# Partial sums of spectral products and of right operands: from GpSimd additions on tiles in SBUF to accumulating transfers into DRAM

## The chip, the cores and the metric

The kernel runs on one core of a Trainium2 chip. The time is the device time of one execution in microseconds (us). Before the change three executions took 2755.38, 2753.51 and 2754.12 us, a median of 2754.12 us. The core's engines are TensorE (PE, with its weight loads as PEld), VectorE (DVE), ScalarE (ACT), GpSimd (POOL) and SyncE (SP); each works through its own queue in order and waits for the others by semaphores.

## What is computed

Two sublayers stand side by side, and their outputs are concatenated along the last axis: multi-query attention with 32 heads of width 32 over 2048 tokens, and a Fourier mixing layer, which is a DFT over the hidden axis followed by the real part of a DFT over the sequence axis.

```python
def _A_ref(x, wq, wk, wv, wo):
    q = (x @ wq).reshape(B, S, H, Dh).transpose(0, 2, 1, 3)
    k = x @ wk
    v = x @ wv
    scores = einsum("bhqd,bkd->bhqk", q, k) * (Dh ** -0.5)
    p = softmax(scores, axis=-1)
    o = einsum("bhqk,bkd->bhqd", p, v)
    return o.transpose(0, 2, 1, 3).reshape(B, S, H * Dh) @ wo

def _B_ref(x, dft_seq_re, dft_seq_im, dft_hid_re, dft_hid_im):
    a = einsum("bsd,ed->bse", x, dft_hid_re)
    b = einsum("bsd,ed->bse", x, dft_hid_im)
    return einsum("ts,bse->bte", dft_seq_re, a) - einsum("ts,bse->bte", dft_seq_im, b)

return concatenate([_A_ref(...), _B_ref(...)], axis=-1)    # S=2048, D=1024, float32
```

## The kernel before

**The work.** One program holds both sublayers, and TensorE takes turns between them. The attention runs in 32 units (4 blocks of 512 queries by 8 groups of 4 heads). A unit has 32 steps. In a step a *row* (two products of 512 columns into `pss`) gives scores whose maximum DVE takes (`nm`) and whose sum of exponentials ACT takes; a *column* (two products into `pst`) gives the transposed scores, which ACT turns into `p`. After some steps a *burst* multiplies several chunks of `p` with `v` into a bank `psb`. The method `pv` issues a burst whole, or in two halves (its argument `part`) with a row and a column in between.

Between rows and columns stand the *products* of the projections and of the mixing layer, all into two banks called `psb`. Each operand is split into a rounded high part and a low part (`rh`, `rl` for right operands, `mh`, `ml` for left ones), and each product is three matmuls: high by high, high by low, low by high. DVE makes the high parts (`rounded`, a TENSOR_REDUCE), GpSimd most low parts (a subtraction of 1.3 us).

**The seven products of Strassen's scheme.** The mixing layer's two DFTs (`stage_1`, `stage_2`) and most of the output projection (`stage_3`) are done as two-by-two block products with seven instead of eight block multiplications, listed in `PRODUCTS`. So many operands are sums or differences of two blocks, and each product is added to or subtracted from one or two blocks of the result.

- Sums of results: `gather` evicts a bank into a tile `h` (a ring of three, `NHR`), on DVE. The first product of a result block is stored as it is. For a later one SP loads the block's partial sum from DRAM into a tile `y` (a ring of four, `NY`), GpSimd adds or subtracts `h`, and SP stores `y` again. The intermediate `a` (result of stage 1) lives in `a_d`, that of stage 2 in `y_d` until its last addition, which is stored to the output.
- Sums of right operands: `sum_up` loads two blocks into the tiles `r0` and `r1`, GpSimd adds or subtracts them, and SP stores the result to a scratch in DRAM (`as_...` for stage 2, `ws_...` for stage 3). When TensorE needs the operand, `prepare` loads it from there. Right operands of stage 1 and all left operands are summed in SBUF, in `prepare`.

**What sets the order.** The order of every engine's queue is written out when the program is built, by a planner (`Plan`). Each piece of work is a task with a planned duration, an engine and a priority; `run` picks, for the engine that is free first, the ready task of least priority, and `finish` passes its planned end to the tasks that depend on it. The main loop places TensorE's rows, columns, bursts and products at the planned times at which their inputs are there. So a changed planned duration of one task moves instructions on all engines. The planner's figures (`MM`, `ISSUE`, `FLIGHT`, ...) only set the order; on the chip, semaphores decide. All calls go through one line of the class `Ordered`, so nearly all rows of the profile have line L58, and one tells them apart by tiles.

Of the kernel before, what the change touches and what calls it, by code (L numbers as in the profile page):

```python
# [12 lines left out]
ALU = mybir.AluOpType  # L13
# [4 lines left out]
P = 128  # L18
S = 2048
D = 1024  # L20
H = 32
DH = 32
W = 512
# [20 lines left out]
EXTRA = 2  # L44
OVER = {"act": 0.1, "dve": 0.08, "pool": 0.06, "sp": 0.0}
LAG = {"act": 0.1, "dve": 0.1, "pool": 0.15, "sp": 0.3, "pe": 0.1}
ISSUE, RATE, FLIGHT = 0.42, 300.0, 3.0


class Ordered:  # L50
# [16 lines left out]
class Plan:  # L67
# [6 lines left out]
        self.port = {"dve": 0.0, "pool": 0.0}  # L74
        self.seq, self.dma = 0, 0.0

    def task(self, engines, us, emit, deps=(), prio=0.0, kb=0, order=(), into=None, port=False):
        if isinstance(engines, str):
            engines = ((engines, 0.0),)
        t = into or Task()  # L80
        t.engines, t.us, t.emit, t.prio, t.kb, t.port = engines, us, emit, prio, kb, port
        self.seq += 1
        t.seq = self.seq
        for kind, ds in ((0, deps), (1, order)):
            for d in ds:
                if d is None:
                    continue
                if d.end is None:
                    t.n += 1
                    d.outs.append((t, kind))  # L90
                else:
                    t.ready = max(t.ready, d.start if kind else d.end)
        if t.n == 0:
            self.learn(t)
        return t
# [23 lines left out]
    def run(self, until):  # L119
        while True:  # L120
            best = self.next()
            if best is None or best[0] > until:
                return
            at, e = best
            r, t = min((x for x in self.known[e] if x[0] <= at), key=lambda x: (x[1].prio, x[1].seq))
            for f, _ in t.engines:
                self.known[f] = [x for x in self.known[f] if x[1] is not t]
            t.on = e
            t.emit(e) if len(t.engines) > 1 else t.emit()
            us = t.us[e] if isinstance(t.us, dict) else t.us  # L130
            if e == "pool" or (e == "dve" and t.port):
                at = max(at, self.port["dve" if e == "pool" else "pool"])
                self.port[e] = at + us - OVER[e]
            end = at + us
            self.free[e] = max(end - OVER[e], at + us / 2)
            if e == "sp":
                self.dma = max(self.dma, end) + t.kb / RATE
                end = self.dma + FLIGHT
            self.finish(t, at, end)


class Slot:
# [45 lines left out]
def tile_kernel(ctx: ExitStack, tc, xT, wq, wkv, wo, xbT, wT, cT, out):  # L188
# [8 lines left out]
    plan = Plan()  # L197
# [62 lines left out]
    def maker(ring, *a, **k):  # L260
        t = plan.task(*a, order=ring.maker, **k)
        ring.maker = [t]
        return t
# [87 lines left out]
    def gather(g, at, outs, neg=False):  # L351

        s = hr.take()

        def evict():
            h = hr.make(s)
            if neg:
                dve.tensor_scalar_mul(h, g.ps, -1.0)
            else:
                dve.tensor_copy(h, g.ps)  # L360
        e = g.freed = maker(hr, "dve", 0.69, evict, deps=[g.done, *s.deps], prio=-0.5)
        for sg, key, n, to, of in outs:
            if of is None and sg > 0:
                s.users.append(store(to, lambda: s.tile, [e], at, key=(*key, n)))
                continue
            if of is None:
                s2 = hr.take()
                g.freed = maker(hr, "dve", 0.69, lambda s2=s2: dve.tensor_scalar_mul(hr.make(s2), g.ps, -1.0),
                                deps=[g.done, *s2.deps], prio=-0.5)
                s2.users.append(store(to, lambda s2=s2: s2.tile, [g.freed], at, key=(*key, n)))  # L370
                continue
            ys = yr.take()
            ld = plan.task("sp", ISSUE, lambda ys=ys, of=of: sp.dma_start(yr.make(ys), of()),
                           deps=[landed[*key, n - 1], *ys.deps], prio=at - 30, kb=256, order=yr.maker)
            yr.maker = [ld]
            f = gp.tensor_add if sg > 0 else gp.tensor_sub
            ad = plan.task("pool", 1.33, lambda ys=ys, f=f: f(ys.tile, ys.tile, s.tile), deps=[e, ld], prio=at - 20)
            s.users.append(ad)
            ys.users.append(store(to, lambda ys=ys: ys.tile, [ad], at, key=(*key, n)))

    def stage_1():
        seen = {}
# [22 lines left out]
    def stage_2():  # L405
        seen = {}
        for p in ORDER_2:
# [4 lines left out]
            for m in range(8):  # L412
# [3 lines left out]
                for i, j, sg in outs:  # L416
                    n = seen[i, j, m] = seen.get((i, j, m), 0) + 1
                    r0 = (i * 8 + m) * P
                    to = out[r0:r0 + P, D + j * W:D + (j + 1) * W] if n == TOTAL[i, j] else y_d[i][j][m]
                    got.append((sg, ("y", i, j, m), n, lambda to=to: to,  # L420
                                (lambda i=i, j=j, m=m: y_d[i][j][m]) if n > 1 else None))
                yield Group(L, R, lambda g, at, got=got: gather(g, at, got))

    def wo_set(e):
# [162 lines left out]

    def sum_up(it, at):

        slots = [raw["r"][a].take() for a in range(2)]  # L590
        t = [None, None]
        loads = []
# [602 lines left out]
```

## Time and profile before

| | before |
|---|---|
| median of three executions | 2754.12 us |
| the profiled execution, its own time | 2754.33 us |
| its span, first to last instruction | 2752.5 us |
| granted TensorE clock, mean | 0.999 |
| stage 1: first to last store of `a` begins | 353.6 to 1028.1 us |
| stage 2: first load of `y` to the last addition on `y` begins | 1063.7 to 2478.9 us |

The span leaves out 1.8 us around the first and last instruction. Busy shares are of the span; a matmul's end is modelled, so that matmuls which follow each other closely overlap in the records, and the spacing of their starts says more than their durations: products of 512 columns start every 0.23 us. Issuing a DMA does not count as busy time of an engine.

### The profile page before, as it was taken

What the parts mean: (1) busy time and instruction counts of PE and PEld (TensorE: products, weight loads), DVE (VectorE), ACT (ScalarE), POOL (GpSimd) and SP (SyncE); (2) the same over time, 40 slices, a digit from 0 to 9 for tenths busy, and PEclk for the clock granted to TensorE, in tenths of its full rate; (3) what the DMA queues carried; (4) which work ended last, traced back from release to release, by engine and by line L of the source; (5) the groups of instructions that cost most, each with busy time, mean ns of one, the idle gap of its engine ahead of it and who ended that gap; (6) DMA issues with size and microseconds to landing.
All of it is one profiled execution on the core that took longest, in us unless ns stands there. A gap on an engine that the chain in (4) does not pass through costs nothing.

```text
span 2752.5 us, 40883 instructions
## 1 busy us (share of the span) xinstructions
PE 2736.0 (99%) x13832; PEld 1930.3 (70%) x13832; DVE 1944.1 (71%) x2277; ACT 2199.5 (80%) x3197; POOL 1579.5 (57%) x1307
## 2 busy tenths in 40 slices
PE   9999999999999999999999999999999999999999
PEld 6777676767676767677677676676676776766766
DVE  8977676768777776676677677677677676678752
ACT  6688887878787878888888888888888888887631
POOL 2644245557776557556346356557768767555562
PEclk9999999999999999999999999999999999999999
DMA  9645366567786548547437445547858857444585
GB/s 279 210 135 159 104 202 207 191 231 256 249 257 222 169 149 281 171 133 250 141 106 249 143 136 174 154 153 254 272 182 279 278 161 238 127 127 153 160 277 176
DMA packets 337043, 536.48 MB, mean 195 GB/s; under 512 B 36800, under 2 KB 89536, under 8 KB 336832
## 3 DMA queue, kind: packets, MB, share of 16 engines
q1 hardware_dynamic: 336832, 533.87, 61.3%
q8 instruction: 108, 1.77, 0.3%
q14 instruction: 103, 0.84, 0.1%
HBM read 390.86 MB, written 141.82 MB: 194 GB/s over the span
## 4 chain that ended last, share of the span: by engine, by line
PE 97%; ACT 1%; DVE 1%; DMA 1%; issue 0%; POOL 0%; SPq 0%; ACTq 0%; DVEq 0%
PE psb L58 62%; PE pss L58 18%; PE pst L58 17%; ACT pss L58 0%; ACT p L58 0%; DMA qst<-in_xT_dram 0%; DVE h L58 0%; DMA ql<-y 0%; DVE nm L58 0%; DVE rl L58 0%; DMA m<-in_wkv_dram 0%; DVE y L58 0%; ACT h L58 0%; POOL rl L58 0%; DVE p L58 0%
## 5 line engine op out<-in xcount | busy, mean ns | idle before, releaser
L58 DVE TENSOR_REDUCE nm<-pss 128x1 f32<-128x1024 f32 x1024 | 1241.6, 1221 | 325.0 <-PE pss L58 321.2
L58 ACT ACTIVATE p<-pst 128x1024 f32<-128x1024 f32 x1024 | 1052.5, 1028 | 448.6 <-PE pst L58 397.7
L58 ACT ACTIVATE pss<-pss,nm 128x1024 f32<-128x1024 f32 x1024 | 1110.7, 1085 | 35.0 <-DVE nm L58 33.6
L58 POOL TENSOR_TENSOR ml<-m,mh 128x512 fp32r<-128x512 f32 x371 | 482.6, 1301 | 508.2 <-DVE mh L58 290.9
L58 PE MATMUL psb<-rl,mh 128*128 128x512 f32 x1732 | 683.3, 395 | 0.6 <-POOL rl L58 0.6
L58 PE MATMUL psb<-rh,mh 128*128 128x512 f32 x1732 | 683.7, 395 | 0.2 <-DVE y L58 0.2
L58 PE MATMUL psb<-rh,ml 128*128 128x512 f32 x1732 | 683.3, 394 | 0.0
L58 PE MATMUL pss<-kst,qst 128*128 128x512 f32 x2048 | 650.4, 398 | 0.9 <-ACT pss L58 0.9
L58 PE MATMUL pst<-qst,kst 128*128 128x512 f32 x2048 | 642.8, 395 | 2.4 <-ACT p L58 2.2
L58 PEld LDWEIGHTS pss<-kst,qst 128*128 128x128 f32 x2048 | 375.6, 188 | 163.6 <-issue 72.9
L58 PE MATMUL psb<-p,v 128*32 128x512 f32 x4096 | 461.8, 596 | 2.7 <-DVE h L58 2.7
L58 PEld LDWEIGHTS pst<-qst,kst 128*128 128x128 f32 x2048 | 382.5, 188 | 103.1 <-ACT p L58 8.6
L58 POOL TENSOR_TENSOR m<-m,m 128x512 f32<-128x512 f32 x230 | 301.0, 1309 | 152.4 <-DMA m<-in_cT_dram 93.8
L58 PEld LDWEIGHTS psb<-rh,mh 128*128 128x128 f32 x1732 | 324.9, 188 | 77.7 <-DVE y L58 0.6
L58 PEld LDWEIGHTS psb<-rl,mh 128*128 128x128 f32 x1732 | 324.9, 188 | 76.6 <-POOL rl L58 1.0
L58 PEld LDWEIGHTS psb<-rh,ml 128*128 128x128 f32 x1732 | 324.9, 188 | 75.7
L58 POOL TENSOR_TENSOR y<-y,h 128x512 f32<-128x512 f32 x192 | 249.3, 1306 | 176.8 <-DVE h L58 165.1
L58 PEld LDWEIGHTS psb<-p,v 128*32 128x32 f32 x4096 | 122.7, 110 | 286.5 <-issue 273.7
L58 POOL TENSOR_TENSOR rl<-r,rh 128x512 fp32r<-128x512 f32 x198 | 255.7, 1299 | 117.6 <-DVE rh L58 108.5
L58 DVE TENSOR_REDUCE mh<-m 128x512 fp32r<-128x512 f32 x371 | 250.7, 676 | 20.5 <-PE psb L58 13.8
L58 ACT ACTIVATION_READ_ACCUMULATOR pss<-pss,nm 128x1 f32 x1024 | 208.2, 203 | 0.0
L58 POOL TENSOR_TENSOR r<-r,r 128x512 f32<-128x512 f32 x140 | 180.5, 1293 | 47.8 <-DMA r<-a 31.1
(78 smaller groups left out, 977.0 us busy)
## 6 DMA issues: line engine op xcount, KB each, us to landing
m<-in_cT_dram SPq DMA_DIRECT2D x384, 256.0 KB, 3.8
r<-a SPq DMA_DIRECT2D x192, 256.0 KB, 4.2
y<-a SPq DMA_DIRECT2D x128, 256.0 KB, 3.7
a<-y SPq DMA_DIRECT2D x128, 256.0 KB, 3.2
r<-in_wT_dram SPq DMA_DIRECT2D x96, 256.0 KB, 3.9
m<-in_xbT_dram SPq DMA_DIRECT2D x96, 256.0 KB, 3.3
y<-y SPq DMA_DIRECT2D x96, 256.0 KB, 4.1
as<-r SPq DMA_DIRECT2D x80, 256.0 KB, 4.4
```

What stands on the lines that cost most here:

```text
L58: return lambda *a, **k: self.tc.keep_in_program_order(f(*a, **k))
```

## The change

In `gather` the load into `y`, the addition on GpSimd and the store are replaced by one transfer that GpSimd issues: it takes the tile `h` from SBUF and adds it to the block in DRAM (`accum_op=ALU.add`). Since it only adds, a product that is subtracted is evicted a second time, negated, into another tile `h`. The partial sums of stage 2 go to the output itself from the first product on, so that `y_d` is no longer used. In `sum_up` a sum with a plus sign becomes a copy from DRAM to DRAM that SP issues and an accumulating transfer from DRAM to DRAM on GpSimd; sums with a minus sign stay as they were. The planner gets a figure `ACC` for an issue on GpSimd, and `after`, a time by which a task's planned end lies behind the engine's part of it.

```diff
-ISSUE, RATE, FLIGHT = 0.42, 300.0, 3.0
+ISSUE, RATE, FLIGHT, ACC = 0.42, 300.0, 3.0, 1.0
...
-            self.finish(t, at, end)
+            self.finish(t, at, end + t.after)
...
-            ys = yr.take()
-            ld = plan.task("sp", ISSUE, lambda ys=ys, of=of: sp.dma_start(yr.make(ys), of()),
-                           deps=[landed[*key, n - 1], *ys.deps], prio=at - 30, kb=256, order=yr.maker)
-            yr.maker = [ld]
-            f = gp.tensor_add if sg > 0 else gp.tensor_sub
-            ad = plan.task("pool", 1.33, lambda ys=ys, f=f: f(ys.tile, ys.tile, s.tile), deps=[e, ld], prio=at - 20)
-            s.users.append(ad)
-            ys.users.append(store(to, lambda ys=ys: ys.tile, [ad], at, key=(*key, n)))
+            if sg < 0:
+                s2 = hr.take()
+                e2 = g.freed = maker(hr, "dve", 0.69, lambda s2=s2: dve.tensor_scalar_mul(hr.make(s2), g.ps, -1.0),
+                                     deps=[g.done, *s2.deps], prio=-0.5)
+            else:
+                s2, e2 = s, e
+            s2.users.append(plan.task("pool", ACC, lambda s2=s2, to=to: gp.dma_start(to(), s2.tile, accum_op=ALU.add),
+                                      deps=[e2, landed[*key, n - 1]], prio=at - 20, into=landed[*key, n], after=FLIGHT + 1.0))
...
-                    to = out[r0:r0 + P, D + j * W:D + (j + 1) * W] if n == TOTAL[i, j] else y_d[i][j][m]
+                    to = out[r0:r0 + P, D + j * W:D + (j + 1) * W]
                     got.append((sg, ("y", i, j, m), n, lambda to=to: to,
-                                (lambda i=i, j=j, m=m: y_d[i][j][m]) if n > 1 else None))
+                                True if n > 1 else None))
...
     def sum_up(it, at):
 
+        kept, key = it.sums, (it,)
+        if it.srcs[1][1] > 0:
+            (ap, _), (bp, _) = it.srcs
+            plan.task("sp", ISSUE, lambda: sp.dma_start(kept, ap(), max_dma_last_dim=2048), deps=[landed[it.after[0]] if it.after else at_group[at - 480].done],
+                      prio=at - 100, kb=256, into=landed[key, 0])
+            plan.task("pool", ACC, lambda: gp.dma_start(kept, bp(), accum_op=ALU.add, max_dma_last_dim=2048),
+                      deps=[landed[key, 0], *(landed[k] for k in it.after)], prio=at - 100, into=landed[key], after=FLIGHT + 1.0)
+            it.after, it.srcs = [key], [(lambda: kept, 1)]
+            return
```

Counted in the two programs, instruction by instruction:

| engine | what | before | after |
|---|---|---|---|
| PE | all instructions | 11786 | 11786 |
| PE | bursts on `p` and `v` that stand as one piece, or as a half | 102 | 96 |
| POOL | additions `y<-y,h` | 192 | 0 |
| POOL | sums `r<-r,r` | 140 | 80 |
| POOL | low parts `ml`, `rl` | 569 | 575 |
| POOL | accumulating transfers | 0 | 252 (192 from `h`, 60 from DRAM) |
| DVE | negated evictions `h<-psb` | 56 | 80 |
| DVE | low parts `ml<-m,mh`, `rl<-r,rh` | 69 | 63 |
| SP | issues and the like | 2238 | 1734 |

The planner gives other places to many instructions from about 350 us on. Three places follow.

**GpSimd, in stage 1**, where product 3 of `PRODUCTS` (counted from 0) is added to two result blocks at a time (`a_...` are the blocks in DRAM, `m0`, `m1` and `r0`, `r1` operands that are being summed). Before:

```order
L58 TENSOR_TENSOR y_6312<-y_6312,h_6513 128x512
L58 TENSOR_TENSOR y_6379<-y_6379,h_6513 128x512
L58 TENSOR_TENSOR m0_6436<-m0_6436,m1_6441 128x512
L58 TENSOR_TENSOR y_6478<-y_6478,h_6553 128x512
L58 TENSOR_TENSOR y_6510<-y_6510,h_6553 128x512
L58 TENSOR_TENSOR ml_6573<-m0_6198,mh_6572 128x512
```

And after, at the same place:

```order
L58 DMA a_0_1_0_198<-h_6461 128x512
L58 DMA a_1_1_0_230<-h_6461 128x512
L58 TENSOR_TENSOR ml_6473<-m0_6156,mh_6472 128x512
L58 TENSOR_TENSOR r0_6350<-r0_6350,r1_6405 128x512
L58 DMA a_0_0_1_183<-h_6511 128x512
L58 DMA a_1_0_1_215<-h_6511 128x512
L58 TENSOR_TENSOR rl_6533<-r0_6350,rh_6532 128x512
```

Each addition on a tile `y` has become one issue that reads `h`; both users of one `h` stand next to each other as before, and low parts and operand sums stand between them.

**TensorE, at the end of stage 1** (about 1000 us before the change): one burst. Before, in two halves with a row and a column between them:

```order
L58 MATMUL psb<-rl,mh 128x512
L58 MATMUL psb<-rh,ml 128x512
L58 MATMUL psb<-p,v 32x512 x12
L58 MATMUL pss<-kst,qst 128x512 x2
L58 MATMUL pst<-qst,kst 128x512 x2
L58 MATMUL psb<-p,v 32x512 x12
```

And after:

```order
L58 MATMUL psb<-rl,mh 128x512
L58 MATMUL psb<-rh,ml 128x512
L58 MATMUL psb<-p,v 32x512 x24
L58 MATMUL pss<-kst,qst 128x512 x2
L58 MATMUL pst<-qst,kst 128x512 x2
```

The two halves of 12 have become one burst of 24; the same happens at all six places where a burst stood in halves.

**TensorE, at the end of the attention** (from about 2630 us on). Before, the last columns stand where the products have run out; the last burst and the first output product (`pss<-rh,mh`) follow:

```order
L58 MATMUL pst<-qst,kst 128x512 x2
L58 MATMUL psb<-rh,ml 128x512
L58 MATMUL pst<-qst,kst 128x512 x4
L58 MATMUL psb<-p,v 32x512 x20
L58 MATMUL pss<-rh,mh 128x512
```

After, two columns stand back to back (x4) some 210 rows ahead of the last burst, in the second half of `stage_3`:

```order
L58 MATMUL pst<-qst,kst 128x512 x2
L58 MATMUL psb<-rh,mh 128x512
L58 MATMUL pst<-qst,kst 128x512 x4
L58 MATMUL psb<-rl,mh 128x512
L58 MATMUL psb<-rh,ml 128x512
```

while behind the last column 23 product matmuls are left, of which the last three stand here ahead of the last burst:

```order
L58 MATMUL psb<-rh,mh 128x512
L58 MATMUL psb<-rl,mh 128x512
L58 MATMUL psb<-rh,ml 128x512
L58 MATMUL psb<-p,v 32x512 x20
L58 MATMUL pss<-rh,mh 128x512
```

The pair of columns without a product between them has moved from the very end to a place further ahead.

More of the change, by code (lines that the diff above doesn't have):

```diff
@@ L75, in __init__, with task @@
         self.seq, self.dma = 0, 0.0
-    def task(self, engines, us, emit, deps=(), prio=0.0, kb=0, order=(), into=None, port=False):
+    def task(self, engines, us, emit, deps=(), prio=0.0, kb=0, order=(), into=None, port=False, after=0.0):
         if isinstance(engines, str):
@@ L80, in task @@
         t = into or Task()
-        t.engines, t.us, t.emit, t.prio, t.kb, t.port = engines, us, emit, prio, kb, port
+        t.engines, t.us, t.emit, t.prio, t.kb, t.port, t.after = engines, us, emit, prio, kb, port, after
         self.seq += 1
```

## The prediction

> **What bounds the kernel now.** I read the page's busy shares and its chain first.
>
> ```profile
> PE 2736.0 (99%) x13832; PEld 1930.3 (70%) x13832; DVE 1944.1 (71%) x2277; ACT 2199.5 (80%) x3197; POOL 1579.5 (57%) x1307
> PE 97%; ACT 1%; DVE 1%; DMA 1%; issue 0%; POOL 0%; SPq 0%; ACTq 0%; DVEq 0%
> ```
>
> TensorE is idle for 2752.5 - 2736.0 = 16.5 us, and 97% of the chain that ended last is its own. GpSimd and SP, where the change removes work, have no share of it. A busy PE need not be a dense one, so I looked next at what it waits for, over the whole span:
>
> ```profile
> engine line waited for: us in total, times, longest us
> PE psb L58 <- ACT p L58: 4.8, 1, 4.8
> PE psb L58 <- DVE h L58: 2.7, 4, 0.7
> PE pst L58 <- ACT p L58: 2.2, 3, 1.2
> PE pss L58 <- ACT pss L58: 0.9, 2, 0.7
> PE psb L58 <- DVE p L58: 0.9, 1, 0.9
> PE psb L58 <- POOL rl L58: 0.6, 1, 0.6
> PE psb L58 <- DVE y L58: 0.2, 1, 0.2
> ```
>
> That is 12.3 us. The waits of 4.8 and 0.9 on `p` are in the first 60 us, ahead of everything that the change moves. The one wait on GpSimd is 0.6 us. So all additions that leave GpSimd cost TensorE at most that now. The change has the same 11786 instructions on TensorE, so it can gain only by their order and by some 6 us of later waits; it can lose much more, if a new transfer comes late.
>
> **Term 1: six bursts in one piece, -2.0 us.** The order has 102 pieces of bursts before and 96 after. Two stretches price a piece; the number behind x counts records, two for each matmul:
>
> ```profile
> 1000.61 0.62 PE L58 MATMUL pst<-qst,kst 128*128 128x512 f32 x2
> 1001.16 2.78 PE L58 MATMUL psb<-p,v 128*32 128x512 f32 x24
> 1003.88 0.73 PE L58 MATMUL pss<-kst,qst 128*128 128x512 f32 x2
> 1004.44 0.62 PE L58 MATMUL pst<-qst,kst 128*128 128x512 f32 x2
> ...
> 1314.00 5.36 PE L58 MATMUL psb<-p,v 128*32 128x512 f32 x48
> 1319.29 0.73 PE L58 MATMUL pss<-kst,qst 128*128 128x512 f32 x2
> ```
>
> A half of 24 records takes 2.72 us from start to the next start, a whole burst of 48 takes 5.29; two halves are 0.15 us longer. The pair of matmuls ahead of a burst takes 0.55 us and the one behind it 0.56, instead of 2 x 0.23 = 0.46, which adds 0.09 + 0.10. A split costs 0.34 us, six of them 2.0 us.
>
> **Term 2: one transpose less ahead of a burst, -0.7 us.** All four waits on `h` above are of this kind: a small transpose takes a bank, and a burst behind it waits for the other bank's eviction.
>
> ```profile
> 1024.41 0.27 PE L58 MATMUL psb<-ident,m 128*128 128x128 f32 x1
> 1025.36 2.78 PE L58 MATMUL psb<-p,v 128*32 128x512 f32 x24 [0.68 <-DVE h L58]
> ```
>
> In the order this pair stands four times before, three times after: -0.7 us.
>
> **Term 3: the back-to-back columns, 0.** The end of the attention before:
>
> ```profile
> 2694.19 0.62 PE L58 MATMUL pst<-qst,kst 128*128 128x512 f32 x2
> 2694.65 0.40 PE L58 MATMUL psb<-rh,ml 128*128 128x512 f32 x1
> 2695.92 0.72 PE L58 MATMUL pst<-qst,kst 128*128 128x512 f32 x2 [0.88 <-ACT p L58]
> 2697.82 1.11 PE L58 MATMUL pst<-qst,kst 128*128 128x512 f32 x2 [1.17 <-ACT p L58]
> ```
>
> With one product between them these columns start 1.73 us apart, without one 1.90; there is only one tile `pst`, which ACT must empty. Dense, the starts would be 0.69 and 0.46 apart, so that 1.04 + 1.44 = 2.5 us are lost. After the change 23 products, 5.3 us, stand behind the last column, and this loss is gone from the end. But the same pattern (a column, one product, two columns) now stands some 210 rows earlier, for the same 2.5 us. I count 0, between -2.5 (should inputs on the chip space the earlier pair out anyway) and +1.2 (the wait of 0.6 on `rl`, which falls in the same half of stage 3, once or twice more).
>
> **Term 4: GpSimd's issues, 0.** The prices, and the densest stretch, by all work and by that on `y` alone:
>
> ```profile
> L58 POOL TENSOR_TENSOR y<-y,h 128x512 f32<-128x512 f32 x192 | 249.3, 1306 | 176.8 <-DVE h L58 165.1 <-DMA y<-a 6.9 <-issue 2.1
> L58 POOL TENSOR_TENSOR r<-r,r 128x512 f32<-128x512 f32 x140 | 180.5, 1293 | 47.8 <-DMA r<-a 31.1 <-DMA r<-in_wT_dram 9.6 <-DMA r<-in_wo_dram 2.1
> 600.00:700.00 100.00, 100.00 (x516) 69.44 (x515) 74.12 (x92) 80.56 (x120) 70.11 (x59) 1.00 0.72 236
> 700.00:800.00 100.00, 100.00 (x497) 72.28 (x495) 78.03 (x84) 86.07 (x125) 76.73 (x63) 1.00 0.81 258
> 800.00:900.00 100.00, 99.33 (x515) 69.46 (x514) 71.26 (x83) 78.70 (x114) 67.24 (x55) 1.00 0.71 228
> ...
> 600.00:700.00 100.00, 0.00 (x0) 32.98 (x26) 1.00 0.72 236
> 700.00:800.00 100.00, 0.00 (x0) 40.42 (x32) 1.00 0.81 258
> 800.00:900.00 100.00, 0.00 (x0) 31.66 (x24) 1.00 0.71 228
> 702.12 0.32 SPq L58 DMA_DIRECT2D y<-a  x1
> ```
>
> GpSimd loses 192 x 1.306 + 60 x 1.293 = 328 us and gains six low parts (7.8 us) and 252 issues. No row shows an issue by GpSimd. From below SP's 0.32 us bounds it; from above nothing does, so I take the price at which it begins to hurt: between 700 and 800 us GpSimd does 76.7 - 40.4 = 36.3 us of other work, and 32 issues fill the rest at 63.7 / 32 = 2.0 us each. I take 1.3, the nearest row of its own; then GpSimd is as busy as now, and TensorE waits no more than now. At 0.32 it would gain at most the 0.6 us.
>
> A queue effect comes with it. An accumulating transfer from DRAM waits in GpSimd's queue for SP's copy to land, and low parts wait behind it. The additions that it replaces already wait for landings (31.1 us on `r<-a` in the row above), and TensorE felt 0.6. Twice that is +0.6, inside the range.
>
> **Term 5: DVE, 0; SP, 0.**
>
> ```profile
> L58 DVE TENSOR_SCALAR h<-psb 128x512 f32<-128x512 f32 x56 | 38.4, 687 | 12.5 <-PE psb L58 12.0 <-issue 0.4 <-POOL y L58 0.2
> L58 DVE TENSOR_TENSOR rl<-r,rh 128x512 fp32r<-128x512 f32 x54 | 57.5, 1067 | 2.0 <-ACT rh L58 1.5
> L58 DVE TENSOR_TENSOR rl<-qst,rh 128x512 fp32r<-128x512 f32 x6 | 3.9, 682 | 1.5 <-ACT rh L58 1.5
> ```
>
> DVE gets 24 negated evictions, 16.5 us, and loses four low parts of 1.07 and two of about that, some 6 us. The other 10 us lie in its 808 idle us; without that cover they would be +10 us. SP issues 504 fewer DMAs at 0.32 us and more, which nothing waits for.
>
> **Term 6: the DMA engines, 0.**
>
> ```profile
> q1 hardware_dynamic: 336832, 533.87, 61.3%
> y<-a SPq DMA_DIRECT2D x128, 256.0 KB, 3.7
> a<-y SPq DMA_DIRECT2D x128, 256.0 KB, 3.2
> as<-r SPq DMA_DIRECT2D x80, 256.0 KB, 4.4
> ```
>
> 533.87 MB took 61.3% of 2752.5 us, so 256 KB take 0.83 us of all sixteen engines. 192 loads, 192 stores and 60 sums of three transfers go, 564; 60 copies and 252 accumulates come. From below an accumulate costs one such transfer. From above I again take the price that hurts: between 700 and 800 us, 64 of the replaced transfers are 53 of the 81 busy us, and 32 accumulates fill the 72 us that are then free at 2.25 us each, 2.7 transfers. I take two transfers, since an accumulate must read the block in DRAM that the load of `y` read: the load stays unchanged (312 - 252 + 504 = 564).
> The Trainium skill, "Collectives: The Full Stack", section "The bandwidth ceiling", says that an adding DMA is slower than a copying one because of its second read, not because of the addition, at about half the rate. By one transfer the stretch would be 55% loaded, and I would halve the chance of the DMA rival below; by that rule it is 81% loaded; the sum is 0 by either, and no run here shows it yet.
> As for time to land, an `h` is evicted every 6 us there (two users of each, 32 in 100 us), and the ring has three, so that a landing may take 15 us before DVE waits; SP's take 3 to 5.
>
> **Sum.** 2754.33 (the profiled execution's own time, 1.8 over its span and 0.2 over the median) - 2.0 - 0.7 = 2751.6 us.
>
> **The rivals.** *Slower: GpSimd becomes the bound of stage 1.* It decides from 2.0 us per issue. At 2.5, the three stretches above need 37.1 + 65.0 = 102, 36.3 + 80.0 = 116 and 35.6 + 60.0 = 96 of 100 us: +18 us, 2770; at 3.0 they need 115, 132 and 108: +55 us, 2806. For it speaks that a GpSimd instruction pays when DVE reads two operands from SBUF: the same subtraction takes DVE 682 ns at the start and 1067 later, beside a busy GpSimd. Had every issue to sit out one DVE instruction (78.03 / 84 = 0.93 us), it would be 1.3 + 0.9 = 2.2 us: 7 us over in the middle stretch, 2759. Against it: most of DVE's work there are reductions and evictions from PSUM.
> The Trainium skill, "SBUF — State Buffer", section "Who interferes with whom", says that descriptor generation on GpSimd is starved while DVE is in a two-port mode, and that reductions never are. By that rule the price stays near 1.3, since copies here come from PSUM; with it failing for every instruction it is the 2759 above. No run here shows it yet.
> Chance 0.13.
>
> *Slower: an accumulate holds the DMA engines for over 2.7 transfers.* At three (2.5 us) the three stretches come to 29 + 65, 28 + 80 and 31 + 60: +8 us, 2760; at four, +60 us, 2812. Against it: only these 300 us are so dense. Two transfers leave a margin of 2.7 / 2 = 1.35 before it decides; for that, chance 0.07. With a small remainder for a late operand elsewhere (+6 to +10, such as DVE's 10 us uncovered) 0.03.
>
> *Faster: every wait behind the first 60 us goes as well.* Term 3 gives -2.5, the other three transposes -2.0, `rl`, `pss` and `y` -1.6: 2751.6 - 6.1 = 2745.5. It needs all of them; half of them are enough to pass -0.2%. Against it: the pattern of columns is there in the new order. Chance 0.16.
>
> That the additions stay is no rival: the order shows none on `y`.
>
> **How the numbers follow.** The forecast, 2748.6 to 2759.6, has 0.61. About 0.2%, 5.5 us, is what a measurement of this kernel can tell from no change; so faster 0.16, same 0.61, slower 0.13 + 0.07 + 0.03 = 0.23. The range goes from 2746, nearly all of the gains, to 2770, GpSimd at 2.5 us per issue; about 0.12 lie above it and 0.05 below.
>
> **What would show it.** Terms 1 and 2: TensorE's waits on `h` at three times 0.7 us, no burst of 24 records, and 2730 to 2735 us busy. Term 3: starts of columns 1.7 to 1.9 us apart with no product between them some 70 us before the last burst, and none at the end. Term 4: the spacing of GpSimd's issues below 2 us; a wait of TensorE on `rl` or `ml` of more than a few us in stage 1 would prove it wrong. Term 6: a DMA share of at most about 0.8 in the densest stretch, and a share of the whole near 61%; far less would mean that an accumulate costs one transfer, and a full stretch that it costs three.

## The result and the profile after

The changed kernel takes 2774.35 us (median of 4, 2773.15 to 2775.13), the kernel before beside it 2754.75 us. The ratio is 1.0073, with a 95% interval from 1.0061 to 1.0085: 20 us slower, and outside the range of the prediction. Two executions of later versions, at a granted clock of 0.85 and 0.67, are left out of all medians and ratios.

The page of the changed kernel: its span, busy time by engine, DMA share in 40 slices, the queues' shares (queue, packets, MB, share of sixteen engines' span), and the chain by engine.

```profile
span 2773.4 us, 40227 instructions
PE 2741.3 (99%) x13832; PEld 1932.4 (70%) x13832; DVE 1946.5 (70%) x2295; ACT 2197.0 (79%) x3197; POOL 1485.8 (54%) x1313
DMA  9644356769999989647534336566557447445486
q1 hardware_dynamic: 264256, 401.72, 46.8%
q0 software_dynamic: 36288, 66.08, 16.3%
PE 91%; DMA 3%; POOL 2%; DVE 1%; ACT 1%; issue 1%; SPq 0%; POOLq 0%; ACTq 0%; DVEq 0%
```

GpSimd lost 94 us of busy time, as intended. TensorE's part of the chain fell from 97 to 91%, and DMA, which had 1%, has 3. In the slices the row of nines between 620 and 970 us is new. TensorE's waits (what it waited for: us in total, times, longest):

```profile
PE pst L58 <- ACT p L58: 9.9, 6, 3.9
PE pss L58 <- ACT pss L58: 8.7, 9, 2.3
PE psb L58 <- ACT p L58: 5.3, 1, 5.3
PE psb L58 <- DVE h L58: 3.3, 4, 1.3
...
```

With two small ones left out here they sum to 27.8 us, against 12.3 before. None of them names a DMA or GpSimd: it is mostly rows and columns that stand still, not products. The stretches of 100 us show where, and a second loss with it (columns as in the prediction: busy time of PE, PEld, DVE, ACT, POOL, then granted clock, DMA share, GB/s):

```profile
600.00:700.00 100.00, 94.88 (x465) 67.01 (x464) 69.55 (x85) 76.23 (x113) 65.97 (x64) 0.98 0.85 189
700.00:800.00 100.00, 93.16 (x472) 62.41 (x471) 71.09 (x80) 72.29 (x105) 59.90 (x60) 0.97 0.95 203
800.00:900.00 100.00, 97.34 (x482) 69.28 (x481) 70.29 (x82) 82.47 (x121) 66.50 (x65) 1.00 0.95 213
900.00:1000.00 100.00, 99.92 (x514) 69.02 (x514) 68.36 (x81) 81.14 (x118) 63.16 (x63) 1.00 0.95 209
```

TensorE is idle for 14.6 us between 600 and 900 us (0.7 before), and the granted clock is 0.98 and 0.97 in the first two stretches, which is (0.02 + 0.03) x 100 = some 5 us more of lost work. The DMA engines are busy for 85 to 95% where they were at 72, 81, 71 and 55%; up to 900 us they nevertheless move fewer bytes per second.

How a late load becomes a standing column is seen in the chain that ended last (start, us, what), here of the changed kernel ahead of its longest stall in stage 1:

```profile
758.65 7.52 DMA r<-in_wT_dram
...
767.66 7.07 DMA r<-in_wT_dram
...
780.35 0.21 POOL md L58
...
780.72 1.01 ACT p L58
...
781.78 1.22 PE pst L58 x2
```

Two loads that follow each other take 7.5 and 7.1 us, where the median of their kind is 4.2 and was 3.9 before. GpSimd works in order, so all that stands behind the late operand, down to the small `md` that ACT's exponential needs, comes late, and the column on `pst` has waited 3.88 us.

### The profile page after: what moved, and what is told of

It is laid out like the page before. It is cut to its first block, busy times and chain, and to the rows that moved or that the text cites. A ratio compares the mean times of both kernels' runs of the same rounds, so it can differ in the third digit from the quotient of the medians.

```text
span 2773.4 us, 40227 instructions
## 1 busy us (share of the span) xinstructions
PE 2741.3 (99%) x13832; PEld 1932.4 (70%) x13832; DVE 1946.5 (70%) x2295; ACT 2197.0 (79%) x3197; POOL 1485.8 (54%) x1313
## 3 DMA queue, kind: packets, MB, share of 16 engines
q1 hardware_dynamic: 264256, 401.72, 46.8%
q0 software_dynamic: 36288, 66.08, 16.3%
## 4 chain that ended last, share of the span: by engine, by line
PE 91%; DMA 3%; POOL 2%; DVE 1%; ACT 1%; issue 1%; SPq 0%; POOLq 0%; ACTq 0%; DVEq 0%
PE psb L58 58%; PE pss L58 17%; PE pst L58 16%; DMA r<-in_wT_dram 1%; DVE nm L58 1%; ACT pss L58 1%; DMA a<-h 0%; DMA r<-as 0%; POOL r L58 0%; ACT p L58 0%; POOL a L58 0%; POOL ml L58 0%; POOL rl L58 0%; DVE h L58 0%; DMA r<-in_wo_dram 0%
## 5 line engine op out<-in xcount | busy, mean ns | idle before, releaser
L58 POOL TENSOR_TENSOR ml<-m,mh 128x512 fp32r<-128x512 f32 x373 | 514.2, 1385 | 506.2 <-DVE mh L58 277.9
L58 POOL TENSOR_TENSOR m<-m,m 128x512 f32<-128x512 f32 x230 | 311.9, 1356 | 188.1 <-DMA m<-in_cT_dram 115.4
L58 POOL TENSOR_TENSOR rl<-r,rh 128x512 fp32r<-128x512 f32 x202 | 269.1, 1350 | 87.0 <-DVE rh L58 80.0
L58 DVE TENSOR_REDUCE rh<-r 128x512 fp32r<-128x512 f32 x237 | 156.8, 677 | 44.9 <-POOL r L58 17.3
L58 POOL DMA_DIRECT2D a<-h x128 | 121.7, 1054 | 104.2 <-DVE h L58 95.0
```

The lines of the kernel that those rows point to most:

```text
L58: return lambda *a, **k: self.tc.keep_in_program_order(f(*a, **k))
```

## The experiments

Each edit is shown against the changed kernel, or against the kernel before where the text says so; a line may be shown from its changed argument on. Four theories are told apart. **L**: the 48 sums for stage 2, which now stand in stage 1, fill the DMA engines. **Q**: SP's and GpSimd's queues stand behind copies and accumulates that wait for each other, whatever the load. **R**: the 192 accumulates from `h` cost by themselves. **P**, first stated for the run in which accumulates are counted, when four runs were known: the order is planned as if accumulates took no time of the DMA engines, so TensorE, DVE and GpSimd are led to inputs that have not landed.

| run | median, us | ratio to before, 95% interval |
|---|---|---|
| the change | 2774.35 | 1.0061 to 1.0085 |
| results only | 2759.06 | 1.0011 to 1.0030 |
| sums only | 2762.02 | 1.0019 to 1.0047 |
| sums held back | 2823.11 | 1.0230 to 1.0261 |
| copy that waits for nothing | 2769.73 | 1.0041 to 1.0071 |
| an eighth of the sums | 2767.07 | 1.0031 to 1.0061 |
| sums paced | 2773.31 | 1.0058 to 1.0089 |
| accumulates counted | 2764.17 | 1.0023 to 1.0048 |
| counted as one transfer | 2766.56 | 1.0031 to 1.0058 |
| later landing only | 2771.09 | 1.0035 to 1.0067 |
| paced and counted | 2759.65 | 1.0012 to 1.0031 |
| results only, counted | 2752.57 | 0.9986 to 1.0004 |
| before, planned blind | 2755.95 | 0.9997 to 1.0016 |
| results only, four `h` | 2757.76 | 1.0004 to 1.0023 |
| counted, four `h` | 2757.84 | 1.0005 to 1.0023 |
| paced, counted, four `h` | 2760.83 | 1.0012 to 1.0030 |
| results only, counted, four `h` | 2750.52 | 0.9978 to 0.9996 |
| results only, counted, five `h` | 2763.61 | 1.0020 to 1.0045 |
| before, four `h` | 2767.76 | 1.0037 to 1.0062 |

The kernel before took 2753.45 to 2754.75 us beside them.

### The two halves of the change

Results only: `sum_up` as before the change.

```diff
-        kept, key = it.sums, (it,)
-        if it.srcs[1][1] > 0:
...
-            return
         slots = [raw["r"][a].take() for a in range(2)]
```

> Partial results are accumulated in DRAM as in the changed kernel, the sums of right operands stay in SBUF as before. In the changed kernel the 48 sums of stage 2 run at 677 to 1063 us, within stage 1; before they ran from 1039 us on. Theory L (these early sums fill the DMA engines: 48 x (0.85 + 1.79) = 127 us of all sixteen, share 0.95) and theory Q (SP's queue stands behind copies that wait for an accumulate's landing, 163 us) both expect 2752 +- 4 us and a DMA share of about 0.8 at 700 to 800 us. Theory R (the 192 accumulates from h are what delays the loads, 5.5 us to land) expects 2768 to 2776.

Sums only: `gather`, and the place in DRAM of stage 2's partial results, as before the change.

```diff
-            s2.users.append(plan.task("pool", ACC, lambda s2=s2, to=to: gp.dma_start(to(), s2.tile, accum_op=ALU.add),
...
+            ld = plan.task("sp", ISSUE, lambda ys=ys, of=of: sp.dma_start(yr.make(ys), of()),
...
+            ad = plan.task("pool", 1.33, lambda ys=ys, f=f: f(ys.tile, ys.tile, s.tile), deps=[e, ld], prio=at - 20)
...
```

> The sums of right operands are formed in DRAM as in the changed kernel, the partial results by loads, GpSimd additions and stores as before. Theory R expects 2752 +- 4. Theory L expects 2765 to 2775, since a load and a store (1.7 us of all sixteen engines) take about what an accumulate takes (1.8), with the sums still early. Theory Q expects a part, 2757 to 2768: the copies now wait for plain stores, which land in 3.2 us and not 5.5.

They took 2759.06 and 2762.02 us: 5.6 and 8.6 us over the kernel before. Results only lies between the ranges that the theories gave it; sums only lies in that of Q. Together 14 of the 20 us, so each half costs, and both in the same stretch seem to cost more (the intervals do not quite exclude a plain sum). The loss of the first is mainly in two places, at 562 and 664 us, and DVE's timeline in the version with results only shows the first (start, us, instruction, and in brackets the idle time ahead and what ended it):

```profile
553.14 0.68 DVE L58 COPY h<-psb 128x512 f32<-128x512 f32 x1
553.74 0.68 DVE L58 TENSOR_SCALAR h<-psb 128x512 f32<-128x512 f32 x1
554.59 0.69 DVE L58 COPY h<-psb 128x512 f32<-128x512 f32 x1 [0.17 <-DMA a<-h]
...
562.01 0.69 DVE L58 TENSOR_SCALAR h<-psb 128x512 f32<-128x512 f32 x1 [3.82 <-DMA a<-h]
```

Three evictions within 1.5 us take all three `h`. The fourth, a negated one, needs the `h` of an accumulate that was issued at 554.7 and lands 7.2 us later. DVE stands for 3.82 us, and TensorE waits for the bank:

```profile
562.76 0.50 PE L58 MATMUL psb<-rh,mh 128*128 128x512 f32 x1 [2.00 <-DVE h L58]
...
565.26 0.63 PE L58 MATMUL psb<-rh,mh 128*128 128x512 f32 x1
565.69 0.63 PE L58 MATMUL psb<-rl,mh 128*128 128x512 f32 x1
```

The prediction allowed a landing 15 us before DVE would wait, reckoned on one `h` every 6 us. Here a plain and a negated eviction follow each other in 0.6 us, and a landing of 7.2 us was too long. Behind the stall of 2.00 us the starts are 0.43 us apart instead of 0.23, for some 3 us, and the granted clock from 560 to 580 us is 0.91: it is halved for that time. So a stall of 2 us cost nearly 4.

### Sums held back, copies without a wait, an eighth of the bytes

Held back: the sums for stage 2 are not made before 480 groups ahead of their use.

```diff
-deps=[landed[it.after[0]] if it.after else at_group[at - 480].done],
+deps=[*([landed[it.after[0]]] if it.after else []), at_group[at - 480].done],
```

> Both parts of the change, but a stage-2 sum may begin only 480 product matmuls ahead of its first use (the rule that stage 3's sums have), so that all 48 fall into stage 2. Theories L and Q expect 2752 +- 4, with no stall of TensorE above 1 us between 550 and 900 us. Theory R expects 2768 to 2776. A price of an accumulating transfer from DRAM that hurts wherever it stands would move the stalls to 1100 to 2000 us.

It took 2823.11 us, the slowest of all. The sums of a product all become ready in one moment there, and the DMA engines are full at once (a stretch of 20 us, and the chain up to it):

```profile
2100.00:2120.00 20.00, 9.65 (x34) 7.35 (x33) 6.76 (x8) 8.17 (x13) 8.92 (x8) 0.69 1.00 264
```

```profile
2087.97 10.36 DMA as<-a
...
2098.41 13.88 DMA r<-as
...
2112.31 0.69 DVE rh L58
...
2115.48 1.22 PE pss L58 x2
```

A copy takes 10.4 and a load 13.9 us. DVE's rounding of that operand stands in front of the row's maximum `nm`, and the row waits. So the expectation missed: late in the program the sums did more harm, not less, because they came in bunches.

A copy that waits for nothing: the order is that of the changed kernel, but SP's copy reads an input, so the 48 sums take another first operand than the computation asks for. GpSimd's accumulate still waits for the copy and for its own block.

```diff
+it.after_0 = bool(it.after)
...
-sp.dma_start(kept, ap(), max_dma_last_dim=2048)
+sp.dma_start(kept, (xT[0, 0] if it.after_0 else ap()), max_dma_last_dim=2048)
```

> As the changed kernel, in the same order on TensorE, but the first operand of each stage-2 sum is copied from an input instead of from the result a, so that SP's copy waits for no accumulate; the sums are then not those of the reference. The DMA load is the same. Theory Q expects 2752 to 2760, with SP's waits on a<-h (163 us) gone. Theory L expects 2768 to 2776.

An eighth of the bytes: the accumulates of the 48 sums add 16 of 128 rows and leave out the rest.

```diff
+it.stage2 = bool(it.after)
...
-gp.dma_start(kept, bp(), accum_op=ALU.add, max_dma_last_dim=2048)
+gp.dma_start(*((kept[:16], bp()[:16]) if it.stage2 else (kept, bp())), accum_op=ALU.add, max_dma_last_dim=2048)
```

> TensorE's order is that of the changed kernel. Left out: the accumulating transfers of the 48 sums for stage 2 add only 16 of 128 rows, so these sums are incomplete. At 1.79 us of all sixteen DMA engines each in the changed kernel, 48 x 7/8 x 1.79 = 75 us of transfer time go from 650 to 1060 us, all else stands. Load theory (the early sums fill the DMA engines): the DMA share of 700 to 1000 us falls from 0.95 to about 0.8, most of the 20 us goes, 2757 to 2764. Queue theory (SP's copies and GpSimd's accumulates stand in front of loads and low parts, however short they are): 2767 to 2773, since the same instructions wait in the same places.

They took 2769.73 and 2767.07 us. With the copy that waits for nothing, SP's waits on `a<-h` between 600 and 1100 us fell from 163 to 27 us, and 5 of 20 us came back (Q); the intervals of loss, 17 to 23 and 11 to 20 us, still overlap. Taking away some 70 us of transfer time (L) brought the share between 700 and 900 us from 0.95 to 0.86 and 0.88, and 7 us back. Each lies outside the range that its own theory gave it: neither is the cause by itself.

### Sums paced

Two sums at a time, spread over stage 2:

```diff
-deps=[landed[it.after[0]] if it.after else at_group[at - 480].done],
+deps=[*([landed[it.after[0]]] if it.after else []), at_group[at - 480 if not it.after else at_group[at].at - 480 + 8 * (at - at_group[at].at)].done],
```

> The changed kernel, but the 48 sums for stage 2 are released two at a time, a pair every 8 product matmul groups from 480 groups ahead of their use, instead of as soon as their blocks are there or sixteen at once. Load theory: spread over stage 2, whose DMA share is about 0.5, 127 us of transfers hurt nothing, and the time is that of the kernel with accumulated results only, 2756 to 2761. Rival, a price that is paid wherever a sum stands (a copy and an accumulate take the place of an addition, and something in order waits behind them): 2766 to 2774, with stalls spread over stage 2.

2773.31 us: nothing gained, so L in its simple form falls. In its trace (of an execution of 2781.13 us, the longest of four) the stalls of stage 1 at 562 and 665 us stayed, those from 700 to 900 us went, and new ones came at 1441 to 1468 and at 2094 to 2128 us. The chain ahead of the longest new one:

```profile
2108.03 8.08 DMA ws<-r
...
2116.18 8.17 DMA r<-as
...
2124.37 0.69 DVE rh L58
...
2128.14 1.22 PE pss L58 x2
```

It is the picture of the changed kernel once more: a store and a load of 8 us one behind the other, then DVE in order, then ACT, then TensorE. Three different places for the same 48 sums, and each time the planner had TensorE ready for an operand that was still on its way.

### What the plan knows

The planner lets SP's transfers queue for the DMA engines (`self.dma`); a task on GpSimd never enters there. Counted:

```diff
                 end = self.dma + FLIGHT
+            elif t.after:
+                self.dma = max(self.dma, end) + 2 * 256 / RATE
+                end = self.dma
             self.finish(t, at, end + t.after)
```

> The changed kernel, but with a planner that counts each accumulate as two transfers of 256 KB in its picture of the DMA engines, as SP's transfers are counted; in the order that comes out, no two columns stand back to back, and the 102 pieces of bursts of before are back. Theory that the loss is a matter of order (TensorE is led to inputs that are not there yet): the stalls of stage 1 shrink, 2755 to 2763. Load theory: the same transfers are asked for in the same 300 us; the engines are as full and 2766 to 2776 stays.

The same three lines in the version with results only and in the one with paced sums:

> Accumulated results only, sums of operands in SBUF, planned with each accumulate counted as two transfers. Theory P (what costs time is an order that was planned without the accumulates' hold on the DMA engines, so that TensorE is led to inputs before they have landed): most of the 5.6 us of the uncounted version (2759.1) goes, 2752 to 2756. Theory L (the transfers themselves): 2757 to 2761 as before, since the same bytes are moved in the same stretch.

> The version with stage 2's sums paced in pairs (2773.3), planned with each accumulate counted as two transfers. P: the stalls at 540, 660, 1460 and 2120 us shrink, 2757 to 2763. A price that is paid wherever a sum stands, whatever the plan: 2769 to 2776.

They took 2764.17, 2752.57 and 2759.65 us, the last two inside P's ranges and the first 1 us above. Nothing but the order was changed by it, and 10 of 20, all of 5.6 and 14 of 19 us came back. The pair with results only is the cleanest. The same stretch, first with accumulates uncounted, then counted:

```profile
540.00:560.00 20.00, 20.00 (x108) 13.58 (x107) 16.77 (x22) 14.85 (x22) 13.35 (x11) 1.00 1.00 258
560.00:580.00 20.00, 18.00 (x72) 14.10 (x70) 14.91 (x17) 15.68 (x23) 11.57 (x10) 0.91 0.76 197
```

```profile
540.00:560.00 20.00, 20.00 (x108) 13.56 (x107) 16.94 (x23) 14.71 (x22) 12.54 (x11) 1.00 0.99 251
560.00:580.00 20.00, 20.00 (x88) 16.17 (x87) 17.82 (x20) 19.67 (x28) 15.72 (x14) 1.00 0.89 233
```

The DMA engines are as full in the first 20 us of both, and only the uncounted one stalls behind them. DVE's timeline of the counted one tells why:

```profile
559.23 0.69 DVE L58 TENSOR_TENSOR ov<-ov,psb 128x512 f32<-128x512 f32 x1 [1.69 <-PE psb L58]
559.87 2.36 DVE L58 TENSOR_REDUCE nm<-pss 128x1 f32<-128x1024 f32 x2
562.14 0.68 DVE L58 TENSOR_SCALAR h<-psb 128x512 f32<-128x512 f32 x1
```

The negated eviction runs at the same time as before, 562.14 us against 562.01. But the planner, which now expected a late `h`, put an eviction of `ov` and two maxima ahead of it. In the uncounted order DVE does nothing between 558.2 and 562.0 us, and the next maximum starts at 563.2. Here nobody waits.

The reverse, the kernel before the change, planned as if the loads of `y` and their stores took no DMA time:

```diff
-deps=[landed[*key, n - 1], *ys.deps], prio=at - 30, kb=256, order=yr.maker)
+deps=[landed[*key, n - 1], *ys.deps], prio=at - 30, kb=0, order=yr.maker)
...
-ys.users.append(store(to, lambda ys=ys: ys.tile, [ad], at, key=(*key, n)))
+ys.users.append(store(to, lambda ys=ys: ys.tile, [ad], at, kb=0, key=(*key, n)))
```

> The kernel before the change, with no accumulating transfer in it, but planned with the 192 loads of y and their 192 stores counted as no load on the DMA engines. On the chip they move as many bytes as before. P: TensorE is led to inputs too early, as in the changed kernel, and stalls appear between 500 and 1000 us: 2759 to 2775. Rival, the accumulates' own price (double hold of the engines, longer landings) is what costs: there is none here, 2752 to 2756.

2755.95 us, no measurable loss; here P missed, and the rival that was named with it, a price of the accumulates themselves, had it in its range. That rival fails in turn at results only, counted, where all 192 accumulates stand and nothing is lost. The plan left out 384 x 0.83 = 319 us of transfers, much as with results only (192 x 1.81 = 348 us, from 12.6% of 2758.9 us), and lost a third as much. So a blind plan is not enough by itself. It takes landings that something close to TensorE waits for: an accumulate holds `h`, which DVE needs to empty a bank, while in the kernel before a landing held only a `y`, and `h` was free after GpSimd's 1.3 us. This last step, which speaks of the results and not of the sums, is argued from the rows above and was not tried by itself.

### Hold or landing

Is it the hold on the engines that the plan must know, or only the later landing? Once with 8 us planned from issue to landing instead of 5 and no hold, once with a hold of one transfer:

```diff
-after=FLIGHT + 1.0
+after=FLIGHT + 4.0
```

> The changed kernel, with the accumulates planned to land 3 us later (8 us behind the start of the issue instead of 5; 5.5 is the measured median), but still without a hold on the DMA engines that SP's transfers stand behind. If any other order would do as well as the counted one, or if the landing of the accumulates themselves was planned too early: 2758 to 2766, as with counting (2764.2). If what is missing is the hold on the loads beside them: 2769 to 2777.

```diff
-                self.dma = max(self.dma, end) + 2 * 256 / RATE
+                self.dma = max(self.dma, end) + 256 / RATE
```

> The changed kernel, with each accumulate counted as one transfer of 256 KB in the planner's picture of the DMA engines. Between uncounted (2774.4) and counted as two (2764.2), if the loss goes with the time that the plan leaves out: 2767 to 2771. 2764 if any hold will do, 2774 if one is not enough.

2771.09 us, with runs from 2763 to 2773 us, and 2766.56 us, the first where it was expected if the hold is what the plan lacks, the second just below the 2767 to 2771 that were expected of one transfer. By the ratios the loss is 20, 12 and 10 us with no, one and two transfers counted, and 14 us with a later landing alone. So it falls as the plan leaves out less, though 12 and 10 are not told apart. The later landing gave back less than the hold, but its interval (10 to 18 us) overlaps that of one transfer (9 to 16). So this points to the hold and does not settle it.

### What is left, and a version that beats both

Counting left 9.5 us in the full change. Its stretches with three `h`:

```profile
700.00:800.00 100.00, 99.17 (x501) 69.95 (x494) 74.91 (x84) 79.27 (x115) 65.42 (x66) 1.00 1.00 216
800.00:900.00 100.00, 94.63 (x479) 62.53 (x481) 67.03 (x77) 74.08 (x110) 67.03 (x65) 1.00 0.94 215
```

The DMA engines are all but full for 200 us and more, since the 48 sums are still there, and this order does not hide that wholly. That L is what is left was not tested. TensorE's waits on `h` were 6.8 us, so a fourth `h` was tried, in the room of a `y`, in five versions: results only; counted; paced and counted; results only and counted; and the kernel before.

```diff
-    NY, NHR, NP, NQS = 4, 3, 6, 3
+    NY, NHR, NP, NQS = 3, 4, 6, 3
```

> The kernel with accumulated results only (sums of operands in SBUF as before the change), but with four tiles h instead of three, and three tiles y instead of four for their room. Ring theory: its remaining loss, 2759.1 against 2753.5, is DVE waiting for an h that an accumulate still reads, at about 560 and 660 us; with a fourth h those two stalls go and the time is 2750 to 2755. Load theory: the accumulates hold up loads whatever the ring is, 2757 to 2761.

> The changed kernel, planned with each accumulate counted as two transfers, and with four tiles h (and three y). With three h the counted version took 2764.2, and TensorE waited 6.8 us for an h. Ring theory: those waits go, 2757 to 2760. Otherwise 2762 to 2766.

> Both parts of the change, sums of stage 2 in pairs, accumulates counted as two transfers, four tiles h and three y. With three h it took 2759.7; a fourth h was worth 6 us where sums stand in stage 1, 0 to 1 in the version with accumulated results only. 2755 to 2759; below 2753 it would beat the kernel before.

> Accumulated results only, counted as two transfers, four tiles h and three y; 97 pieces of bursts instead of 102 before the change. With three h it took 2752.6 (102 pieces). If a split burst costs 0.34 us, as the prediction had it: 2750 to 2752, ratio 0.998 to 0.9995. If the splits are hidden: 2752 to 2754.

> The kernel before the change, with no accumulating transfer, but with four tiles h and three y. Its order has 97 pieces of bursts, as the best version so far (2750.5). If that version's gain is the fourth h and the whole bursts that come with it, this one has it too: 2750 to 2752. If accumulates are needed for it, because here every load and store of a result's sum needs one of only three y: 2753 to 2758.

2757.76, 2757.84, 2760.83, 2750.52 and 2767.76 us; the third and the last are outside what was expected. A fourth `h` is worth 6 us where the sums fill stage 1 and the plan counts, with these sums left where they are, so that of the 9.5 us some 4 are left; 2 us with results only and counted, where the intervals overlap; and nothing measurable without counting or with paced sums. In the kernel before it costs 13 us; that this is for want of the fourth `y` was not shown. With two `y` and five `h` the best version turns bad as well:

```diff
-    NY, NHR, NP, NQS = 3, 4, 6, 3
+    NY, NHR, NP, NQS = 2, 5, 6, 3
```

> Accumulated results only, counted as two transfers, five tiles h and two y, 97 pieces of bursts. If the ring of h still holds TensorE up at four, 2748 to 2750; if four are enough, as three stalls of 0.7 us on an h say, 2750 to 2752, the same as with four.

2763.61 us, far above both ranges, with a wait that is at most 0.2 us in the others (from its longest execution, 2768.79 us):

```profile
PE psb L58 <- DVE y L58: 9.8, 3, 5.2
```

The version with results only, counted, four `h` is 4.1 us faster than the kernel before, and its interval, 0.9978 to 0.9996, lies below 1. It is small, and it lies in the better of the two ranges that were expected; it shows that accumulating transfers need not cost.

## Why the prediction was wrong

**Terms 1 and 2.** As forecast in the order: no burst stands in halves. The price of a split was not measured alone. Results only, counted, went from 102 pieces of bursts to 97 and gained 2.0 us with the fourth `h`, which agrees with 5 x 0.34 = 1.7, but a tile changed too. TensorE waited 3.3 us on `h` instead of three times 0.7. Its busy time is 2741.3 us, not 2730 to 2735, since matmuls at half clock count as busy.

**Term 3.** The pattern came where it was expected (TensorE's timeline of the changed kernel):

```profile
2651.04 0.73 PE L58 MATMUL pst<-qst,kst 128*128 128x512 f32 x2 [0.25 <-ACT p L58]
2651.96 0.49 PE L58 MATMUL psb<-rh,mh 128*128 128x512 f32 x1 [0.19 <-DVE rh L58]
2652.89 0.74 PE L58 MATMUL pst<-qst,kst 128*128 128x512 f32 x2 [0.43 <-ACT p L58]
2654.80 1.22 PE L58 MATMUL pst<-qst,kst 128*128 128x512 f32 x2 [1.17 <-ACT p L58]
2655.82 0.63 PE L58 MATMUL psb<-rl,mh 128*128 128x512 f32 x1
2656.25 0.63 PE L58 MATMUL psb<-rh,ml 128*128 128x512 f32 x1
```

Columns without a product between them start 1.91 us apart, and the end is free of it. Behind the last of these columns matmuls start 0.43 us apart for some 3 us. By the starts, 4.5 us are lost between 2640 and 2660 us.

The prediction counted 2.5 us for the pattern, on both sides. In the kernel before it also cost more than that, because the burst behind the columns was slowed:

```profile
2698.86 5.72 PE L58 MATMUL psb<-p,v 128*32 128x512 f32 x40
2704.52 0.50 PE L58 MATMUL pss<-rh,mh 128*128 128x512 f32 x1
```

A burst of the same size in the changed kernel, a little ahead of the pattern:

```profile
2640.55 4.50 PE L58 MATMUL psb<-p,v 128*32 128x512 f32 x40
2644.98 0.73 PE L58 MATMUL pst<-qst,kst 128*128 128x512 f32 x2
```

From start to start the first took 5.66 us and the second 4.43, and the granted clock before was 0.50 from 2698 to 2700 us. With 0.5 us of the pair ahead of the burst, the loss before was 2.5 + 0.5 + 1.2 = 4.2 us. So the term is +0.3 us, close to the 0 that was forecast, but both of its sides were taken too small: that they cancel is luck.

**Term 4.** Right, and a little dear. GpSimd's groups in the changed kernel (on GpSimd, other than on SP, these rows count an issue as busy; busy time, mean ns, idle time ahead and what ended it):

```profile
L58 POOL DMA_DIRECT2D a<-h x128 | 121.7, 1054 | 104.2 <-DVE h L58 95.0 <-DVE mt L58 5.9 <-DVE l L58 2.3
L58 POOL DMA_DIRECT2D as<-a x48 | 47.5, 1077 | 57.3 <-DMA as<-a 39.4 <-DMA a<-h 9.3 <-DMA r<-in_wT_dram 4.4
```

An issue takes 1.05 us, where 1.3 was taken and 2.0 would have decided; the rival of a bound GpSimd is refuted. The Trainium skill's rule on a starved descriptor generation ("SBUF — State Buffer", "Who interferes with whom") found no case: the median issue is 0.89 us, and only single ones reach 2.1. What the queue effect had at +0.6 is the row of 39.4 us in which GpSimd stands for SP's copies, and it was larger. With the copy that waits for nothing it was 19.5 us, and 5 us came back.

**Term 5.** DVE's busy time rose by 2 us and hurt nothing as an amount. Its order did: the negated evictions wait for an `h`.

**Term 6 failed.** Its price was right: 16.3% of 2773.4 us for 252 accumulates is 1.79 us each, 2.1 times the 0.85 us of a plain transfer (46.8%, 401.72 MB). The Trainium skill's rule of about half the rate ("Collectives: The Full Stack", "The bandwidth ceiling"), which the page states for the adding transfers of a collective, agrees with the trace. The share of the whole, 46.8 + 16.3 = 63%, is near the 61% that the term named. Three things around the price were wrong.

First, the amount in the stretch. The term expected a share of at most 0.81 between 700 and 800 us, from the 32 accumulates that replace the additions there; with results only it was 0.85, not far off. It left out that the 48 sums for stage 2 move as well. All sums for stage 2 had stood between 1039 and 2194 us, held to the tiles `r` that they needed; as transfers from DRAM to DRAM they need no tile, and stand as soon as their blocks are there (issues on SP, then on GpSimd: times of the first and the last):

```profile
L58 SPq DMA_DIRECT2D as<-a x48: 470/488/668, 649.9 to 1056.8; - x48
...
L58 POOL DMA_DIRECT2D as<-a x48: 807/862/1879, 677.2 to 1062.7; - x48
```

That is 48 x (0.85 + 1.79) = 127 us of all DMA engines more in 400 us, and the share is 0.95. The order of the changed kernel showed it before any run.

Second, the test by a full share. The term let time be lost only where the engines are over 100% busy for 100 us. With results only the mean share from 500 to 600 us is 0.69, but from 540 to 560 us it is 1.00, and DVE's stall begins there, at 558.2 us. Nor does a full share alone cost: counted, it is 0.99 in the same 20 us, and nothing is lost. Loads are late before the mean is full: those of the chain above took 7 to 8 us instead of 4, in a stretch with a share of 0.95.

Third, what sits on a landing. An `h` now waits for one, and the plan did not know of the hold. The 15 us that the term allowed a landing took the evictions as evenly spaced, and left out that a negated product takes a second `h`. Counting gave back 10 of the 20 us, a fourth `h` on top of it 6 more, and with results only counting gave back all of 5.6: so R falls too, since the same 192 accumulates cost nothing there.

Of the rivals, none was the mechanism. The remainder for a late operand, +6 to +10 us with a chance of 0.03, came nearest in kind; a stall can be dearer than its wait, when the clock drops behind it: the waits rose by 15.5 us, and some 5 us of granted clock went with them.

**Still open.** What the last 4 us of the changed kernel are, counted and with four `h`; why the paced and counted version keeps 5.6 us; and whether hold or landing is what the plan must know. Each version has an order of its own, so single differences of 2 to 3 us between versions are not read.

## What to carry to other kernels

When a step loses the tile that paced it, look up in the new order where its transfers went, and add up the DMA time of that stretch, not of the one they left. If an instruction order is planned ahead, give the planner the hold of every new kind of transfer before judging the change: here three lines decided between 5.6 us lost and nothing lost. Accumulating transfers paid where they replace load, addition and store (DMA time of 1.8 instead of 1.7 us each, and a tile less), and not, in these orders, where a copy and an accumulate replace two loads, an addition and a store: with both, counted and with four `h`, 2757.84 us, with results only 2750.52.

## What the runs showed of the hardware

TensorE's granted clock can halve behind short stalls. After a wait of 3.88 us in the changed kernel, matmuls start every 0.43 us instead of 0.23 for some 5 us, and the granted clock from 780 to 800 us is 0.83:

```profile
781.78 1.22 PE L58 MATMUL pst<-qst,kst 128*128 128x512 f32 x2 [3.88 <-ACT p L58]
```

The Trainium skill ("TensorE: Matmul & The Clock Gate", "Part 1: The HAM clock gate") states a half rate after at least one idle window of about 3.4 us. The half rate agrees. The length of the idle time does not: a single wait of 2.00 us was enough at 562.76, at 2654.80 four waits of 0.19 to 1.17 us within 4 us, and before the change two of 0.88 and 1.17 us at its end, where the measurement decides. Such short stalls need not do it: with an eighth of the sums a wait of 1.99 us at 562.52 left the granted clock at 1.00 from 560 to 580 us. So the length of a single wait below some 3 us does not tell what it will cost; the traces do not show what does.

An accumulate of 256 KB from SBUF lands in 5.5 us (median of `a<-h`), one from DRAM in 6.0; beside full DMA engines a copy took 10.4 and a plain load 13.9 us.
